# A batch's 24-point transform on VectorE and GpSimd: another table of steps, both DFT halves in one step, and half of the output subtraction a step sooner

## The chip, the cores and the metric

The kernel runs on one core of one Trainium2 chip. The metric is the device time of one execution in microseconds (us). The profiler's trace of one execution shows each instruction on TensorE (PE, with its weight loads as PEld), VectorE (DVE), ScalarE (ACT), GpSimd (POOL) and the DMA queues (SP issues most of them).

## What is computed

```python
X = np.fft.fft(np.fft.fft(x, axis=1), axis=2).real      # x: 8 x 3072 x 256
x = X.reshape(24576, 256)
h = x @ w_in                                            # w_in: 256 x 2048
x = (h - np.tanh(h)) @ w_out                            # w_out: 2048 x 256
logits = x @ w_gate                                     # 8 experts
out = gate * (relu(x @ w1[e]) @ w2[e])                  # e = argmax(logits), 256 -> 1024 -> 256
```

All of it is fp32; the kernel splits operands into a high and a low part (`hi`, `lo`) and multiplies hi by hi, hi by lo and lo by hi.

## The kernel before

Phase 1 (transform, first dense layer, gating, scattering the rows to the experts) takes some 1960 us, and phase 2 (the experts) the rest. The change touches phase 1 alone.

Phase 1 goes through 24 groups, three for each of the 8 batches; a group is 512 frequencies. A group has 18 steps (`NSTEP`), and the order of every engine's work is the order in which the program issues it. In a step `f` of group `g`:

- TensorE makes `u` and `v` of block `f` (`uv`, L419, 6 matmuls of 128x512), then adds the tanh part of block `f - 1` to four accumulators `acc[i, s]` (`tmm`, L466: 8 matmuls with `hi`, then 4 with `lo`). Steps 16 and 17 have no tanh block: there the last block's accumulation is done, half `i = 0` in step 16 and half `i = 1` in step 17. Step 0 has no `tmm`.
- VectorE makes `us` from `u` (`take_u`, L433), the low part `lo` of the second half of the previous block (`split_lo`, L460), and from `us` and `v` the two halves of `h` (`combine`, L438; in steps 16 and 17 they go into `lin`). `v` of the next step waits for these, since `u` and `v` have one bank each.
- ScalarE takes tanh of both halves twice, as `hi` and as `t` (`tanh`, L448). The second half's `t` goes to the PSUM bank m0 (then it is called `tp`), the first half's to SBUF.
- GpSimd makes the `lo` of the first half. From step 10 on it also finishes and scatters one block of rows of the group before (`rowS`, L601: a small copy and an indirect DMA), and in step 9 it converts the rows' places (`place`, L557), which VectorE computes at the end of that step.

Between groups, `out1(0)` and `out1(1)` (L481) subtract `acc` from `lin` on VectorE, two operations each; both stand in step 0 of the next group. The spectrum for group `g + 1` is made by `dft` (L351): two halves of 16 matmuls (128x128), each followed by a copy on ScalarE (`pqh`) and a subtraction on VectorE (`pql`). The halves stand in steps 0 and 1, and both use the PSUM bank m1; for group 1 they stand in steps 9 and 10 of group 0, and for group 3 in steps 14 and 15 of group 2.

A batch's 24-point transform (`fft_tasks`, L245) has to be done, in SBUF, before the `dft` of its first group. It is a list of operations: 24 pair operations of 128x768 (`two`), four multiply-adds of 128x768 on `y5, y4` and `y7, y6`, and four times `three`, each two operations of 128x512 and then 10 (once 4) smaller ones on VectorE. `when(nb)` (L55) says in which step each operation of batch `nb` is issued, at the end of the step; the dictionary `fq` holds them. From batch 2 on GpSimd does the pair operations and the first two of each `three`. For batch 1, VectorE does 12 of the pair operations and all of `three`. The transform of batch `nb` begins in group `3 nb - 5` and ends in group `3 nb - 2`, so in cycles of three groups; batch 1 has only groups 0 to 2 for it.

Of the kernel before, what the change touches and what calls it, by code (L numbers as in the profile page):

```python
# [9 lines left out]
F32 = mybir.dt.float32  # L10
# [10 lines left out]
P = 128  # L21
B, N, D = 8, 3072, 256
# [13 lines left out]
KF = FF // P  # L36
# [13 lines left out]
NCH = 3  # L50
NGRP = B * NCH
NSTEP = KF + 2


def when(nb):  # L55

    if nb == 1:
        steps = [t for t in range(12, 32) if t != 18]  # L60
        cut = [[32, 33], [33, 34], [37, 38, 39], [40, 42, 43], [44, 45, 46], [47, 48, 49]]
        return 8, [steps[i * 19 // 24] for i in range(24)], [(None, c) for c in cut]

    s = NSTEP * (NCH * nb - 5)
    slots = [s + NSTEP * g + t for g in range(4) for t in (0, 0, 1, 2, 3, 4, 5, 6, 7, 8, 9, 17)]

    slots = [t for t in slots if t >= s + (18 if nb == 2 else 6)]
    two, rest = slots[:18], slots[18:]
    r = two[-1] + 1
    six = [t for t in rest if t > r + 5][:6]  # L70
    q = six[-1] + 1
    end = s + 4 * NSTEP - 1
    half = (r + 6 + q + 1) // 2, (q + 1 + end) // 2
    return s + 1, two + six, [(None, [r, r + 1]), (None, [r + 2, r + 3]),
                              (r + 4, range(r + 5, half[0])), (r + 5, range(half[0], q + 1)),
                              (q, range(q + 1, half[1])), (q + 1, range(half[1], end))]


def parts(kb, ka):
# [108 lines left out]
def phase1(tc, a, bk, zscr, zny, base, small, ngrp=NGRP):  # L188
    nc = tc.nc
    V, S, G, T, Q = nc.vector, nc.scalar, nc.gpsimd, nc.tensor, nc.sync  # L190
    es = ExitStack()
    cp = es.enter_context(tc.tile_pool(name="cp", bufs=1))
    hp = es.enter_context(tc.tile_pool(name="hp", bufs=3))
# [5 lines left out]
    pm = es.enter_context(tc.tile_pool(name="pm", bufs=1, space=PSUM))  # L199
    free_banks = [(pm, "m0"), (pm, "m1")]  # L200
# [24 lines left out]
    tt = cp.tile([P, 2, 3, D], F32, name="tt")  # L225
# [16 lines left out]
        for i in parts:  # L242
            Q.dma_start(y[:, i:i + 5:4], a["x"][b - 1][:, i:i + 5:4])

    def fft_tasks(y, vs, tmp, eng, first=4):  # L245

        w = y.shape[-1]
        h = w // 2  # L250
        out = []

        def two(i, o0, o1, ops, src, k=0):
            e = eng(i, k)
            for o, x, op in zip((o0, o1), src, ops):
                out.append([(w, lambda o=o, x=x, op=op: e.tensor_tensor(o, *x, op))])

        pm_ops = (ALU.add, ALU.subtract)
        for b in range(4):
            t = tmp(b)  # L260
            yy = (y[:, b], y[:, b + 4])
            two(b, t[:, 0], t[:, 1], pm_ops, (yy, yy))
            o = y[:, b:b + 5:4]
            tf = (t[:, :, :, :h], t[:, :, :, h:])
            two(b, o[:, :, :, :h], o[:, :, :, h:], pm_ops, (tf, tf), 1)
        t = tmp(4)
        stt = V.scalar_tensor_tensor

        def each(*ops):
            out.append([(o.free_size(), lambda fn=fn, o=o, x=x: fn(o, *x)) for fn, o, *x in ops])  # L270

        halves = [(slice(0, h), -1.0), (slice(h, w), 1.0)]

        def three(kr, kj, real):
            sl = slice(kr, kj + 1, max(1, kj - kr))

            def x(i, r=None):
                if r is None:
                    return y[:, sl, i, :]
                return y[:, (kr, kj)[r], i, :]  # L280

            e = eng(9, kr)
            v = vs[(kr + 1) // 2 % 2]
            each((e.tensor_tensor, v, x(1), x(2), ALU.subtract), (e.tensor_tensor, x(1), x(1), x(2), ALU.add))
            f2 = [(stt, x(2), x(1), -0.5, x(0), ALU.mult, ALU.add)]
            if real:
                each(*f2, (V.tensor_tensor, x(0), x(0), x(1), ALU.add))
                each(*((V.tensor_scalar, x(1)[:, :, c], v[:, :, c], sg * S3, None, ALU.mult) for c, sg in halves))
                return
            each(*f2, (V.tensor_tensor, x(0, 0), x(0, 0), x(1, 0), ALU.add),  # L290
                 *((stt, x(0, 1)[:, c], x(0, 1)[:, c], sg, x(1, 1)[:, c], ALU.mult, ALU.subtract if sg < 0 else ALU.add)
                   for c, sg in halves))
            each((stt, x(1, 0), v[:, 1], -S3, x(2, 0), ALU.mult, ALU.add),
                 (stt, x(2, 0), v[:, 1], S3, x(2, 0), ALU.mult, ALU.add))
            each(*((stt, x(i, 1)[:, c], v[:, 0, c], (3 - 2 * i) * sg * S3, x(2, 1)[:, c], ALU.mult,
                    ALU.add if sg > 0 else ALU.subtract) for i in (1, 2) for c, sg in halves))

        sub = (ALU.subtract, ALU.subtract)
        s02, s13 = (y[:, 0], y[:, 2]), (y[:, 1], y[:, 3])
        d13 = (y[:, 5], y[:, 7])  # L300
        def two4():
            two(4, t[:, 0], t[:, 1], pm_ops[::-1], (d13, d13))

        if first == 4:
            two4()
        t5 = tmp(5)
        two(5, t5[:, 0], t5[:, 1], (ALU.add, ALU.add), (s02, s13))
        two(6, y[:, 0], y[:, 1], sub, (s02, s13))
        two(7, y[:, 2], y[:, 3], pm_ops, ((t5[:, 0], t5[:, 1]),) * 2)
        if first != 4:  # L310
            two4()

        each((stt, y[:, 5], t[:, 0], C8, y[:, 4], ALU.mult, ALU.add), (stt, y[:, 4], t[:, 0], -C8, y[:, 4], ALU.mult, ALU.add))
        each((stt, y[:, 7], t[:, 1], C8, y[:, 6], ALU.mult, ALU.add),
             (stt, y[:, 6], t[:, 1], C8, y[:, 6], ALU.mult, ALU.subtract))
        three(5, 7, False)
        three(4, 6, False)
        three(2, 3, True)
        three(0, 1, False)
        return out  # L320
# [127 lines left out]
    def tanh(hs, room):  # L448

        out = []  # L450
        for s in range(2):
            hi = sp.tile([P, 512], F32R, tag="hi", name=f"hi{s}")
            t = pm.tile([P, 512], F32, tag="m0", name="tp") if s and room else \
                hp.tile([P, 512], F32, tag=f"t{s}", name=f"t{s}", bufs=2 - s)
            S.activation(hi, hs[s], AF.Tanh)  # L455
            S.activation(t, hs[s], AF.Tanh)  # L456
            out.append((t, hi))
        return out
# [22 lines left out]
    def out1(i):  # L481
        for s in range(2):
            V.tensor_tensor(linb[s][:, i], linb[s][:, i], acc[i, s], ALU.subtract)  # L483
# [456 lines left out]
    z_parts = {0: 1, 2: 2, 4: 3}  # L940
    todo = []
    fq = {}

    th = hl = None
    for g in range(ngrp + 1):
# [2 lines left out]
        late = 0 if last else 2  # L948
        if last:
            free_banks.append((pm, "m0"))  # L950
        if g == 1:
            vvs = [vv, hp.tile([P, 2, D], F32, tag="t1", name="vv1", bufs=1)]
        for f in range(NSTEP):
            if last and f == 9:
                break
# [51 lines left out]
            if not last:  # L1007
                hs = combine(g, f, us, v)
                if g == 0:
                    rest(f, 2)  # L1010
                th = tanh(hs, g > 0 or f > 7) if f < KF else None
            if f == 0 and g > 0:
                out1(0)
                out1(1)
            for half in range(2):
                if nxt and f == ((9, 10) if g == 0 else (14, 15) if g == 2 else (0, 1))[half]:
                    dft(g + 1, half)()
            if g > 0:
                twin = (g - 1) % NCH == 0
                if f == late + 4:  # L1020
# [25 lines left out]

            now = NSTEP * g + f
            for nb in range(1, B):
                if nb * NCH < ngrp and now == when(nb)[0]:
                    load_x(nb)  # L1050
                    fft = fft_tasks(ys[nb], vvs if nb > 1 else [vv, vv], lambda i: tt,
                                    lambda i, k, nb=nb: V if nb == 1 and (i == 9 or i < 4 and k == 0 or i in (6, 7)) else G,
                                    4 if nb > 1 else 5)
                    _, pool, parts_at = when(nb)
                    for t, part in zip(pool, fft):
                        fq.setdefault(t, []).append(part[0][1])
                    rest_of = fft[24:]

                    cuts = [rest_of[:1], rest_of[1:2], rest_of[2:6], rest_of[6:10], rest_of[10:13], rest_of[13:]]
                    for (at, dve), part in zip(parts_at, cuts):  # L1060
                        steps = [x for p in part for x in p]
                        if at is not None:
                            fq.setdefault(at, []).extend(fn for _, fn in steps[:2])
                            steps = steps[2:]
                        size = sum(n for n, _ in steps)
                        done = 0
                        for n, fn in steps:
                            fq.setdefault(dve[done * len(dve) // size], []).append(fn)
                            done += n
            for fn in fq.pop(now, ()):  # L1070
                fn()
    es.close()
# [293 lines left out]
```

## Time and profile before

| | us |
|---|---|
| median of 3 runs | 3112.3 (3109.7 to 3113.9) |
| the profiled execution | 3112.51 |
| its span, first to last instruction | 3110.7 |
| TensorE busy | 3007.3 (97%) |
| VectorE busy | 2224.6 (72%) |
| ScalarE busy | 1632.0 (52%) |
| GpSimd busy | 1412.2 (45%) |

Busy shares are averages over both phases. Matmuls overlap in the records, so a TensorE that is busy can still be later than it need be: how long a group takes is read from the first `u` matmul of its step 0 to that of the next group. These starts cut the windows of the first view below.

### The profile page before, as it was taken

Reading aid. Unit: us, or ns where it says so; the run is one execution under the profiler, and the core shown is the slowest. Engines: PE = TensorE matmul, PEld = TensorE weight load, DVE = VectorE, ACT = ScalarE, POOL = GpSimd, SP = SyncE. Lnnn points to the kernel's source line nnn. Section 1 sums busy time; section 2 is a strip of 40 time slices with the busy share of each in tenths; the row PEclk is TensorE's granted clock in tenths of the full one; section 3 lists DMA queues with packets and bytes.
Section 4 is the critical chain, followed back from the end, with each engine's and each line's share of the span. In section 5 each row is a group of like instructions: output and inputs, shape, how many; then the busy total and the mean of one; then the engine's idle time right before and its main releaser. Section 6 shows DMA issues by size and latency. Waiting matters only on the chain. (4 is left out here: it accounts for less than half of the span.)

```text
span 3110.7 us, 44908 instructions
## 1 busy us (share of the span) xinstructions
PE 3007.3 (97%) x15660; PEld 2500.6 (80%) x15660; DVE 2224.6 (72%) x3925; ACT 1632.0 (52%) x3142; POOL 1412.2 (45%) x1372
## 2 busy tenths in 40 slices
PE   7998999999999999999999999799999999999998
PEld 7776778878778878878878887788888888888886
DVE  7779776777776776776776666776766767667664
ACT  4454545555545555555555555555555555555553
POOL 4466566566566566566554443622222222222222
PEclk8999999999999999999999999899999999999999
DMA  6120121121121121121111111765555556555551
GB/s 181 62 80 24 29 69 35 33 72 35 33 71 34 36 69 36 34 71 36 32 32 36 35 33 32 221 178 157 153 156 158 176 152 164 156 156 164 155 152 40
DMA packets 301614, 278.04 MB, mean 89 GB/s; under 512 B 246046, under 2 KB 261446, under 8 KB 285894
## 3 DMA queue, kind: packets, MB, share of 16 engines
q1 hardware_dynamic: 282422, 222.08, 26.7%
q0 software_dynamic: 18848, 52.99, 4.9%
q8 instruction: 125, 2.05, 0.3%
q14 instruction: 107, 0.88, 0.1%
q10 hardware_dynamic: 112, 0.05, 0.0%
HBM read 168.28 MB, written 55.39 MB: 72 GB/s over the span
## 5 line engine op out<-in xcount | busy, mean ns | idle before, releaser
L455 ACT ACTIVATE hi<-h 128x512 fp32r<-128x512 f32 x768 | 479.3, 624 | 835.9 <-DVE h L444 832.3
L463 POOL TENSOR_TENSOR lo<-t,hi 128x512 fp32r<-128x512 f32 x384 | 507.3, 1321 | 629.3 <-ACT t L456 500.1
L1290 POOL DMA_INDIRECT out_dram<-y,i x200 | 239.9, 1200 | 845.1 <-DVE y L1286 330.2
L435 DVE SCALAR_TENSOR_TENSOR us<-zb,A,u 128x512 f32<-128x512 f32 x432 | 321.8, 745 | 400.9 <-PE u L427 397.1
L1279 PE MATMUL dn<-w2s,hh 128*128 128x512 f32 x1600 | 572.3, 398 | 0.0
L1281 PE MATMUL dn<-w2s,hl 128*128 128x256 f32 x1600 | 449.2, 281 | 0.0
L1279 PEld LDWEIGHTS dn<-w2s,hh 128*128 128x128 f32 x1600 | 300.9, 188 | 69.5
L1266 PE MATMUL up<-xh,w1h 128*128 128x512 f32 (+1 forms) x960 | 344.7, 359 | 9.2 <-ACT xh L1254 9.2
L1267 PE MATMUL up<-xl,w1h 128*128 128x512 f32 (+1 forms) x960 | 341.7, 356 | 1.3 <-DVE xl L1255 1.1
L1268 PE MATMUL up<-xh,w1l 128*128 128x512 f32 (+1 forms) x960 | 342.5, 357 | 0.0
L1285 ACT ACTIVATE y<-dn,gi 128x256 f32<-128x256 f32 x200 | 95.1, 475 | 422.4 <-PE dn L1281 416.3
L1286 DVE SCALAR_TENSOR_TENSOR y<-dn,gi,y 128x256 f32<-128x256 f32 x200 | 96.8, 484 | 300.8 <-ACT y L1285 300.8
L1281 PEld LDWEIGHTS dn<-w2s,hl 128*128 128x128 f32 x1600 | 302.3, 189 | 4.9
L1271 DVE SCALAR_TENSOR_TENSOR hl<-up,hh 128x512 fp32r<-128x512 f32 (+1 forms) x480 | 271.7, 593 | 33.8 <-ACT hh L1270 33.8
L1270 ACT ACTIVATE hh<-up 128x512 fp32r<-128x512 f32 (+1 forms) x480 | 239.4, 521 | 94.1 <-PE up L1268 94.0
L444 DVE TENSOR_TENSOR h<-us,v 128x512 f32<-128x512 f32 x384 | 260.1, 677 | 3.0 <-DVE us L435 0.5
L445 DVE TENSOR_TENSOR h<-us,v 128x512 f32<-128x512 f32 x384 | 260.6, 679 | 0.0
L463 DVE TENSOR_TENSOR lo<-tp,hi 128x512 fp32r<-128x512 f32 x376 | 256.9, 683 | 3.7 <-ACT tp L456 3.7
L475 PE MATMUL acc<-hi,W0a 128*128 128x512 f32 x768 | 249.2, 405 | 0.4
L456 ACT ACTIVATE t<-h 128x512 f32<-128x512 f32 x392 | 241.4, 616 | 0.0
L479 PE MATMUL acc<-lo,W0a 128*128 128x512 f32 x768 | 215.8, 395 | 24.5 <-DVE lo L463 21.1
L475 PE MATMUL acc<-hi,W1a 128*128 128x512 f32 x768 | 238.9, 392 | 0.0
(278 smaller groups left out, 6516.6 us busy)
## 6 DMA issues: line engine op xcount, KB each, us to landing
w<-in_w SPq DMA_DIRECT2D x120, 1024.0 KB
yb<-in_x SPq DMA_DIRECT2D x16, 768.0 KB
ya<-in_x SPq DMA_DIRECT2D x12, 768.0 KB
zb<-zscr SPq DMA_DIRECT2D x24, 256.0 KB
raw<-in_win SPq DMA_DIRECT2D x8, 512.0 KB
raw<-in_wout SPq DMA_DIRECT2D x8, 512.0 KB
out_dram<-y,i POOLq DMA_INDIRECT x200
row<-pl SPq DMA_TRANSPOSE x184
```

The lines of the kernel that those rows point to most:

```text
L435: V.scalar_tensor_tensor(us, zb[g], A128[:, f:f + 1], u, ALU.mult, ALU.add)
L444: V.tensor_tensor(hs[0], us, v, ALU.subtract)
L445: V.tensor_tensor(hs[1], us, v, ALU.add)
L455: S.activation(hi, hs[s], AF.Tanh)
L463: e.tensor_tensor(lo, t, hi.bitcast(F32), ALU.subtract)
L475: T.matmul(acc[i, s], wout(wi, f)[:, c], hl[s][0], start=f == 0 and wi == 0, stop=False)
L1266: T.matmul(ps, w1h[:, k, c], xh[:, k], start=k == 0, stop=False)
L1267: T.matmul(ps, w1h[:, k, c], xl[:, k], start=False, stop=False)
L1268: T.matmul(ps, w1l[:, k, c], xh[:, k], start=False, stop=k == 1)
L1271: V.scalar_tensor_tensor(hl[:, m], ps, 0.0, hh[:, m].bitcast(F32), ALU.max, ALU.subtract)
L1279: T.matmul(ps.rearrange("p a d -> p (a d)"), hh[:, m, c], w2s[:, m].rearrange("p a d -> p (a d)"), start=m == 0, stop=False)
L1281: T.matmul(ps[:, 1], hl[:, m, c], w2s[:, m, 0], start=False, stop=m == 7)
```

## The change

The change replaces `when`, which worked out the steps by rules, by fixed lists of steps for batch 1, batch 2 and the batches from 3 on. From batch 3 on the pair operations stand in steps 17 and 0 to 9, and VectorE's operations in steps 10 to 14. For batch 2 VectorE's stand there too, but for four in steps 4 and 5 of group 3. For batch 1 GpSimd now does all pair operations and the first two of each `three`; VectorE's stand in steps 10 and 11 of group 1 and in steps 2 to 13 of group 2. The second buffer for `three` (`vv1`) is there from batch 1 on.

The second `dft` half moves from step 1 to step 0 and takes the bank m0, where the first keeps m1. For that, the second half's `t` of step 0 goes to SBUF. `out1(0)` moves from step 0 of the next group to step 17. Groups 0 and 2 keep their `dft` steps.

```diff
     if nb == 1:
-        steps = [t for t in range(12, 32) if t != 18]
-        cut = [[32, 33], [33, 34], [37, 38, 39], [40, 42, 43], [44, 45, 46], [47, 48, 49]]
-        return 8, [steps[i * 19 // 24] for i in range(24)], [(None, c) for c in cut]
...
-    return s + 1, two + six, [(None, [r, r + 1]), (None, [r + 2, r + 3]),
-                              (r + 4, range(r + 5, half[0])), (r + 5, range(half[0], q + 1)),
-                              (q, range(q + 1, half[1])), (q + 1, range(half[1], end))]
+        first = [12, 13, 14, 15, 16, 17, 17, 18, 18, *range(19, 28), 30, 32, 34, 35, 36, 36]
+        later = [(None, [28]), (None, [29]), (37, range(38, 41)), (38, range(41, 44)), (41, range(44, 46)), (44, range(46, 50))]
+        return [t + 36 for t in first], [(at and at + 36, [t + 36 for t in dve]) for at, dve in later]
+    if nb == 2:
+        return ([18, 18, 19, 20, 21, 22, 23, 24, 25, 26, 27, 35, 35, 36, 36, 37, 38, 39, 42, 43, 53, 53, 54, 54],
+                [(None, [40]), (None, [41]), (44, range(46, 49)), (45, range(48, 51)), (55, range(64, 66)), (56, range(66, 69))])
+    return ([4, 5, 6, 7, 8, 9, 17, 18, 18, 19, 20, 21, 22, 23, 24, 25, 26, 27, 37, 38, 39, 40, 41, 42],
+            [(None, [28, 29]), (None, [30, 31]), (35, range(46, 49)), (36, range(48, 51)),
+             (54, range(64, 66)), (55, range(66, 69))])
...
-            t = pm.tile([P, 512], F32, tag="m0", name="tp") if s and room else \
-                hp.tile([P, 512], F32, tag=f"t{s}", name=f"t{s}", bufs=2 - s)
+            if s and room:
+                t = pm.tile([P, 512], F32, tag="m0", name="tp")
+            elif s and room is None:
+                t = hp.tile([P, 512], F32, tag="t1", name="t1", bufs=1)
+            else:
+                t = hp.tile([P, 512], F32, tag="t0", name="t0", bufs=2)
...
-                th = tanh(hs, g > 0 or f > 7) if f < KF else None
+                th = tanh(hs, f > 0 if g > 0 else f > 7 or None) if f < KF else None
             if f == 0 and g > 0:
+                out1(1)
+            if f == NSTEP - 1 and not last:
                 out1(0)
-                out1(1)
             for half in range(2):
-                if nxt and f == ((9, 10) if g == 0 else (14, 15) if g == 2 else (0, 1))[half]:
+                if nxt and f == ((9, 10) if g == 0 else (14, 15) if g == 2 else (0, 0))[half]:
+                    if half and f == 0:
+                        free_banks[:] = [(pm, "m0")]
                     dft(g + 1, half)()
+                    free_banks[:] = [(pm, "m1")]
...
-                    fft = fft_tasks(ys[nb], vvs if nb > 1 else [vv, vv], lambda i: tt,
-                                    lambda i, k, nb=nb: V if nb == 1 and (i == 9 or i < 4 and k == 0 or i in (6, 7)) else G,
-                                    4 if nb > 1 else 5)
+                    if nb == 1:
+                        vvs = [vv, hp.tile([P, 2, D], F32, tag="t1", name="vv1", bufs=1)]
+                    first, later = when(nb)
+                    fft = fft_tasks(ys[nb], vvs, lambda i: tt, lambda i, k: G)
```

The numbers in the lists count steps from the first step of group `3 nb - 5`; for batch 1 this comes to steps of the whole kernel (18 is step 0 of group 1, 36 step 0 of group 2). VectorE's operations of a part are spread evenly over its steps, by their number.

## Rows read from the trace of the kernel before

**Rows 1.** Windows by group: start:end, length (us), busy times, clock, DMA share, GB/s:

```profile
166.40:245.50 79.10, 75.26 (x376) 60.33 (x375) 63.05 (x103) 40.63 (x76) 49.38 (x44) 1.00 0.23 71
245.50:336.00 90.50, 79.57 (x377) 61.14 (x378) 82.42 (x135) 40.89 (x77) 54.50 (x45) 0.98 0.11 28
336.00:413.70 77.70, 74.60 (x377) 60.66 (x375) 57.17 (x105) 40.62 (x76) 48.02 (x44) 1.00 0.13 32
413.70:645.10 231.40, 225.71 (x1128) 183.04 (x1127) 174.04 (x317) 122.02 (x229) 150.04 (x135) 0.99 0.17 46
645.10:1566.80 921.70, 900.66 (x4509) 730.62 (x4508) 674.88 (x1245) 487.97 (x916) 578.54 (x525) 1.00 0.17 46
1106.20:1185.80 79.60, 76.49 (x377) 61.86 (x376) 60.20 (x112) 40.62 (x76) 48.32 (x45) 0.98 0.25 71
1645.40:1869.30 223.90, 222.16 (x1129) 182.68 (x1128) 151.46 (x274) 122.02 (x229) 89.75 (x99) 1.00 0.14 33
```

**Rows 2.** Timeline, start of group 21: start us, us, instruction [idle before it]:

```profile
1723.23 0.48 PE L425 MATMUL u<-pqh,Mh 128*128 128x512 f32 x1
...
1723.09 2.47 DVE L483 TENSOR_TENSOR lin<-lin,acc 128x512 f32<-128x512 f32 x4
1726.08 0.73 DVE L435 SCALAR_TENSOR_TENSOR us<-zb,A,u 128x512 f32<-128x512 f32 x1
...
1727.47 0.97 PE L479 MATMUL acc<-lo,W0a 128*128 128x512 f32 x3 [0.56 <-DVE lo L463]
...
1724.77 0.58 ACT L361 ACTIVATE pqh<-dps 128x512 fp32r<-128x512 f32 x1
```

**Rows 3.** Timeline, end of group 12 and start of group 13:

```profile
1103.88 0.28 DVE L270 SCALAR_TENSOR_TENSOR yb<-yb 128x128 f32<-128x128 f32 x1
1106.46 4.03 DVE L270 SCALAR_TENSOR_TENSOR yb<-vv,yb 128x256 f32<-128x256 f32 x1
...
1104.80 1.87 POOL L256 TENSOR_TENSOR yb<-yb 128x768 f32<-128x768 f32 x1
1106.61 3.58 POOL L256 TENSOR_TENSOR yb<-tt 128x768 f32<-128x768 f32 x2
```

**Rows 4.** Timeline, group 2, steps 13 and 14:

```profile
312.82 0.39 PE L425 MATMUL u<-pqh,Mh 128*128 128x512 f32 x1
316.92 0.40 PE L425 MATMUL u<-pqh,Mh 128*128 128x512 f32 x1
321.25 0.96 PE L479 MATMUL acc<-lo,W0b 128*128 128x512 f32 x3 [0.70 <-DVE lo L463]
...
312.13 0.68 DVE L270 SCALAR_TENSOR_TENSOR yb<-yb 128x512 f32<-128x512 f32 x1
314.69 0.73 DVE L435 SCALAR_TENSOR_TENSOR us<-zb,A,u 128x512 f32<-128x512 f32 x1
317.15 2.79 DVE L270 SCALAR_TENSOR_TENSOR yb<-vv,yb 128x256 f32<-128x256 f32 x6
319.86 0.73 DVE L435 SCALAR_TENSOR_TENSOR us<-zb,A,u 128x512 f32<-128x512 f32 x1
...
312.95 1.47 POOL L463 TENSOR_TENSOR lo<-t,hi 128x512 fp32r<-128x512 f32 x1 [0.63 <-ACT t L456]
```

**Rows 5.** Timeline, step 10 of group 7:

```profile
697.56 1.20 PE L479 MATMUL acc<-lo,W0b 128*128 128x512 f32 x4 [0.66 <-POOL lo L463]
```

**Rows 6.** Groups by line, count | busy us, mean ns | idle us before:

```profile
L463 POOL TENSOR_TENSOR lo<-t,hi 128x512 fp32r<-128x512 f32 x384 | 507.3, 1321 | 629.3 <-ACT t L456 500.1 <-issue 103.7 <-POOL tt L256 13.1
L256 POOL TENSOR_TENSOR tt<-ya 128x768 f32<-128x768 f32 x36 | 66.8, 1865 | 1.1 <-DVE yb L270 0.9
L256 DVE TENSOR_TENSOR tt<-yb 128x768 f32<-128x768 f32 x8 | 7.4, 950 | 0.0
L591 POOL DMA_INDIRECT bk<-row,gpi x184 | 182.8, 994 | 52.5 <-POOL row L599 26.4 <-PE v L430 22.7 <-PE acc L475 1.8
L270 POOL TENSOR_TENSOR vv<-ya 128x512 f32<-128x512 f32 x12 | 15.5, 1295 | 3.1 <-DVE ya L270 3.1
```

More of the change, by code (lines that the diff above doesn't have):

```diff
@@ L59, in when @@
     if nb == 1:
-        steps = [t for t in range(12, 32) if t != 18]
-        cut = [[32, 33], [33, 34], [37, 38, 39], [40, 42, 43], [44, 45, 46], [47, 48, 49]]
-        return 8, [steps[i * 19 // 24] for i in range(24)], [(None, c) for c in cut]
[L64 to L73, printed above, removed]
-    return s + 1, two + six, [(None, [r, r + 1]), (None, [r + 2, r + 3]),
-                              (r + 4, range(r + 5, half[0])), (r + 5, range(half[0], q + 1)),
-                              (q, range(q + 1, half[1])), (q + 1, range(half[1], end))]
+        first = [12, 13, 14, 15, 16, 17, 17, 18, 18, *range(19, 28), 30, 32, 34, 35, 36, 36]
[7 more added lines that the diff above has]
+             (54, range(64, 66)), (55, range(66, 69))])
 def parts(kb, ka):
@@ L243, in load_x, with fft_tasks @@
             Q.dma_start(y[:, i:i + 5:4], a["x"][b - 1][:, i:i + 5:4])
-    def fft_tasks(y, vs, tmp, eng, first=4):
+    def fft_tasks(y, vs, tmp, eng):
         w = y.shape[-1]
@@ L300, in fft_tasks @@
         d13 = (y[:, 5], y[:, 7])
[L301 to L305, printed above, removed]
+        two(4, t[:, 0], t[:, 1], pm_ops[::-1], (d13, d13))
         t5 = tmp(5)
@@ L309, in fft_tasks @@
         two(7, y[:, 2], y[:, 3], pm_ops, ((t5[:, 0], t5[:, 1]),) * 2)
-        if first != 4:
-            two4()
         each((stt, y[:, 5], t[:, 0], C8, y[:, 4], ALU.mult, ALU.add), (stt, y[:, 4], t[:, 0], -C8, y[:, 4], ALU.mult, ALU.add))
@@ L942, in phase1 @@
     fq = {}
+    used = {}
     th = hl = None
@@ L950, in phase1 @@
             free_banks.append((pm, "m0"))
-        if g == 1:
-            vvs = [vv, hp.tile([P, 2, D], F32, tag="t1", name="vv1", bufs=1)]
         for f in range(NSTEP):
@@ L1048, in phase1 @@
             for nb in range(1, B):
-                if nb * NCH < ngrp and now == when(nb)[0]:
+                s = NSTEP * (NCH * nb - 5)
+                if nb * NCH < ngrp and now == max(8, s + 1):
                     load_x(nb)
-                    fft = fft_tasks(ys[nb], vvs if nb > 1 else [vv, vv], lambda i: tt,
-                                    lambda i, k, nb=nb: V if nb == 1 and (i == 9 or i < 4 and k == 0 or i in (6, 7)) else G,
-                                    4 if nb > 1 else 5)
[L1054 to L1061, printed above, removed]
+                    if nb == 1:
+                        vvs = [vv, hp.tile([P, 2, D], F32, tag="t1", name="vv1", bufs=1)]
+                    first, later = when(nb)
+                    fft = fft_tasks(ys[nb], vvs, lambda i: tt, lambda i, k: G)
+                    for t, fn in zip(first, (fn for part in fft[:24] for _, fn in part)):
+                        fq.setdefault(s + t, []).append(fn)
+                    for part, (at, dve) in zip((fft[24:25], fft[25:26], fft[26:30], fft[30:34], fft[34:37], fft[37:]), later):
+                        steps = [fn for p in part for _, fn in p]
                         if at is not None:
-                            fq.setdefault(at, []).extend(fn for _, fn in steps[:2])
+                            fq.setdefault(s + at, []).extend(steps[:2])
                             steps = steps[2:]
[L1065 to L1069, printed above, removed]
+                        for i, fn in enumerate(steps):
+                            fq.setdefault(s + dve[i * len(dve) // len(steps)], []).append(fn)
             for fn in fq.pop(now, ()):
```

## The prediction

> **What bounds the kernel now.** I read the windows by group first, then the timelines where a group is longer than its neighbours. TensorE is busy almost throughout, so phase 1 is as long as its matmuls and the waits between them; phase 2 is not touched. Three neighbouring groups without any transform take 223.9 us, 74.6 each. Groups 4 to 6, a first full cycle of a batch, take 231.4; each of the next four takes 921.7 / 4 = 230.4, and nearly all of its excess lies in one group: group 13 takes 79.6, so the other two take 150.8 together, only 1.6 over the plain ones. The first batch has group 1 at 79.1, group 2 at 90.5 and group 3 at 77.7 [rows 1]. What can be gained is these excesses, plus whatever wait a plain group still holds.
>
> A plain group holds one at its start. Step 1 begins at 1723.23, but its us comes only at 1726.08, 2.85 us later, since four subtractions (2.47 us) and pql go ahead of it; the lo matmul then waits for VectorE [rows 2]. How late is too late shows in group 2: in step 13 us comes at 314.69, 1.87 after the step's start at 312.82, and the next step still starts 4.10 later, an undisturbed step; in step 14 us comes 2.94 after the start, and TensorE waits with 0.70 of idle shown [rows 4]. I take the rule: a step loses what us comes later than 1.9 us after its start. For the plain step 1 that is 2.85 - 1.9 = 0.95.
>
> In a group like 13 it is worse. A 128x256 operation of VectorE at 1106.46 takes 4.03 us, because GpSimd operations at 1104.80 and 1106.61 (two, 3.58) run without a gap and it ends only after them [rows 3]. Everything at the group's start is then late.
>
> The Trainium skill (SBUF — State Buffer, "Who interferes with whom") says that a VectorE instruction with two SBUF inputs and a GpSimd instruction that reads SBUF block each other until the first finishes. The trace agrees that they block, but the 4.03 us reach past one GpSimd operation of 1.87 to the end of three. By that wording alone the wait would have been under 1.9 us, and the gain in each of six such groups some 2 us smaller.
>
> **The group's start after the change.** Edits: out1(0) goes to step 17, both DFT halves to step 0, no transform operation of VectorE in steps 15 to 17 and 0 to 9 from batch 3 on. TensorE's and VectorE's work stays the same, only its place changes. For a plain group I shift group 21's rows. Two of the four subtractions (1.24 us) run in step 17, in a gap of VectorE; us of step 0 then comes about 0.4 later, and the tanh chain 0.2 later. ScalarE's first pqh stood at 1724.77 and now at some 1724.9, the second follows at 1725.5, and their two pql end at about 1726.9, so that us of step 1 comes at 1726.85 [rows 2]. Step 1 itself begins 1.7 later (16 matmuls more in step 0), at 1724.9: us is 1.9 late, just inside the rule. Gain 0.95, of which I keep 0.9. Bounds: zero, if the second t, now in SBUF, makes lo wait for GpSimd; 0.95, if not. I take the upper end because the rows have GpSimd done with its pair operations by then. There are 19 such groups, 4 to 22: 17.1 us.
>
> Group 13's excess of 5.0 [rows 1] goes, but for two things. Step 10 still has a GpSimd pair operation behind the conversion of the places, which waits for VectorE: the lo after it comes late, at a loss of 0.9 in the trace (0.66 of it shown as idle) [rows 5]; I put 0.4 of it down to VectorE's operations in front of the conversion, which move away, and keep 0.5 (bounds 0.5 and 0.9). And lo of step 1 may stand behind the last GpSimd operation of three, 0.3. Gain 4.2, in six groups (4, 7, ... 19): 25 us.
>
> **The packed steps 10 to 14.** VectorE's operations start 2.46 after us (314.69 to 317.15) [rows 4]. With us 0.9 after an undisturbed start, they have 0.8 us before GpSimd's next lo, which then blocks them for about 1.1. The list of four (512, 256, 128, 128) is in rows 4: from 312.13 to 314.69, 2.56 us with the block, and us came 1.87 late, no loss. The change puts this list into step 10 of one group and step 12 of another: no loss. Step 12 of the third group gets three 128s in front of it, at 0.2 each (1103.88 and the operation behind it [rows 3]): 0.6 + 2.56 = 3.2, so us comes at 0.9 + 2.46 + 3.2 - 4.1 = 2.5, a loss of 0.6. I take 0.5. Bounds: 0, and 1.8 if a second GpSimd operation gets in between. The middle group keeps 0.4 at step 10. Both groups together stand at 0.9 over plain after, 1.6 before: gain 0.7 a cycle, five cycles, 3.5 us. The x load now has to land two steps sooner, by step 4; it is issued about a DFT half sooner, which I cost at nothing; if it came late, GpSimd's queue and the lo in it would stand still for as long.
>
> **The first batch.** GpSimd takes over 12 pair operations at 1.865 instead of 0.950 and 8 of 512 at 1.295 [rows 6]. In group 1 they fit beside lo (1.32): 79.1 becomes 73.7 plus 0.5 (step 10), 0.2 (two 768s in step 11) and 0.4 (lo of step 1 behind a pair operation), 74.8, a gain of 4.3. Group 3: four pair operations ahead of step 1's lo, so that VectorE's lo meets the fifth, 1.4; two of 1.295 behind the late conversion of step 9 and lo after them, done 4.2 into step 10 and wanted at 3.0, 1.2; steps 5 and 12, 0.7: 77.0, a gain of 0.7.
>
> Group 2 gets worse. From step 16 of group 1 GpSimd has queued: lo 1.3, two rows at 1.3 to 1.5 (the scatter alone is 0.994 [rows 6]), two pair operations, then four more in step 0: 15.5 us before the lo of step 1 can begin; with that lo it ends at 16.8. TensorE wants it after 2.7 + 2.9 + 1.4 for the three short steps, 1.3 of waits for VectorE and 3.3 within step 1: 11.6. Loss 5.2, and the 1.3. Steps 1 and 2 then carry 1.32 + 2 x 1.295 + 1.865 = 5.8 each against 4.1: with blocking by VectorE's operations 4.5 together. In steps 5 to 9 VectorE's lists lie again beside pair operations, each operation letting one of GpSimd pass: 9. Sum 20, and 1 for a clock that may fall in the first wait (in group 2 the windows show 0.98 already [rows 1]). On 74.0 that makes 95.5, 5 more than before. Bounds: 86, if the backlog drains as queued and VectorE's lists slip between; 104, if they don't. The three groups: -4.3 + 5.0 - 0.7 = 0. Groups 0 and 23 and the way into phase 2, where TensorE has Nyquist work beside the subtractions, stay.
>
> **Sum.** 17.1 + 25 + 3.5 + 0 = 45.6. The profiled execution took 3112.51, 0.2 above the median. 3112.5 - 45.5 = 3067.
>
> **The rivals.** *The start's wait stays.* The second t of step 0 in SBUF makes that lo a two-input operation, and it meets a GpSimd operation in most groups. For it: 4.03 us [rows 3]. Against: in the reckoning GpSimd is done just before. Price 0.95 in 19 groups and 0.5 more in half of them, 23 us: 3090.
>
> *The packed lists don't fit.* If each list also waits for the row's copy and scatter (0.99 [rows 6]) behind lo, a list of four loses 1.2 and the long one 2.5 or more: 5 a cycle, 25 us: 3092. Against: in step 13 of group 2 the last operations came before the scatter.
>
> *The slower engine's rule.* All of the added GpSimd time lies on the path: 12 x 0.915 + 8 x 0.6 = 16 us: 3083. For it: group 2. Against: GpSimd is busy 49 of 79 us in group 1 [rows 1]. The Trainium skill (GPSIMD Engine Reference, "Engine selection") gives this as a rule, elementwise work on VectorE, GpSimd being about two times slower for two inputs; the trace agrees on the ratio, 1.865 to 0.950.
>
> *Slower.* GpSimd becomes the bound at the group's start: in steps 17 and 0 it has rows and three pair operations before step 1's lo. By the rows' prices that lo ends some 2.4 us before TensorE wants it. Only if GpSimd is over 5 us later than that does each of 18 groups lose 2.6 and more, which eats all 46: 3114 to 3130.
>
> *No change.* The waits removed come back in steps 10 to 14 and group 2 in full: 3112.
>
> **Chances and range.** Forecast 0.64, start's wait 0.12, packed lists 0.09, slower engine's rule 0.06, slower 0.05, no change 0.04. About 0.2% (6 us) is what a measurement of this kernel can tell from no change: faster 0.91, same 0.04, slower 0.05. The forecast's own bounds: group 2 at 86 and no loss in step 12, 12 us less, to which I add 7 for the clock and starts that are better than plain: 3048. Upwards the first three rivals belong inside: 3094.
>
> **What would show it.** In the profile after: plain groups at 73.7, with the first lo matmul of step 1 not waiting; every third group at 74.5 instead of 79.6, and no VectorE operation of 4 us; step 12 before the last lists' group with a wait of about 0.5; group 2 longer than 90, its step 1 waiting 5 us for GpSimd. It is wrong if plain groups stay at 74.6, if a cycle stays above 226, or if group 2 is shorter than before.

## The result, and the profile after

The changed kernel takes 3067.24 us (median, 3065.23 to 3069.22) against 3111.0 of the kernel before beside it: a ratio of 0.9859, 95% interval 0.9842 to 0.9876. The forecast was 3067. The profiled execution took 3069.22 us with a span of 3067.4; of its 43.3 us less, 41.2 lie in groups 4 to 22, 0.9 in groups 1 to 3 and 1.2 behind group 22.

The windows of the changed kernel, columns as in [rows 1]: groups 1, 2, 3, then 7 to 18, 13, 14 and 15 alone, and 20 to 22.

```profile
166.40:241.10 74.70, 74.27 (x376) 60.53 (x375) 54.74 (x97) 40.52 (x76) 58.16 (x48) 1.00 0.24 73
241.10:336.90 95.80, 80.33 (x378) 61.79 (x377) 76.92 (x126) 41.04 (x77) 71.53 (x58) 0.96 0.12 28
336.90:412.80 75.90, 74.58 (x377) 60.53 (x376) 65.81 (x116) 40.50 (x76) 51.53 (x46) 1.00 0.15 33
636.80:1531.60 894.80, 890.90 (x4509) 728.81 (x4508) 677.67 (x1245) 486.78 (x916) 584.01 (x524) 1.00 0.18 48
1084.20:1158.90 74.70, 74.33 (x376) 60.56 (x375) 56.89 (x107) 40.57 (x76) 47.02 (x43) 1.00 0.26 75
1158.90:1233.30 74.40, 74.29 (x379) 61.02 (x379) 54.09 (x96) 40.65 (x77) 51.92 (x46) 1.00 0.16 34
1233.30:1308.00 74.70, 74.19 (x377) 60.63 (x376) 58.38 (x111) 40.52 (x76) 47.03 (x45) 1.00 0.15 34
1605.80:1827.20 221.40, 221.40 (x1129) 182.81 (x1129) 151.69 (x274) 121.69 (x229) 89.71 (x99) 1.00 0.15 34
```

Against [rows 1]: three plain groups 221.4 instead of 223.9, group 13 74.7 instead of 79.6, four cycles 894.8 instead of 921.7. Groups 1 to 3 take 246.4 together, 247.3 before: group 2 pays 5.3 of what groups 1 and 3 gain.

The start of group 21, which answers to [rows 2]: TensorE's first u and first lo matmul of step 1, VectorE's pql and us, ScalarE's pqh (start, us, idle before in brackets).

```profile
1684.63 0.48 PE L413 MATMUL u<-pqh,Mh 128*128 128x512 f32 x1
1687.90 1.07 PE L471 MATMUL acc<-lo,W0a 128*128 128x512 f32 x4
...
1685.33 1.29 DVE L350 TENSOR_TENSOR pql<-dps,pqh 128x512 fp32r<-128x512 f32 x2 [1.01 <-ACT pqh L349]
1686.54 0.74 DVE L423 SCALAR_TENSOR_TENSOR us<-zb,A,u 128x512 f32<-128x512 f32 x1
...
1684.72 1.06 ACT L349 ACTIVATE pqh<-dps 128x512 fp32r<-128x512 f32 x2
```

us comes 1.91 after the step's start, where it was 2.85, and the lo matmul waits for nothing. But ahead of pql VectorE is idle for 1.01: there it waits for ScalarE, no longer for the subtractions.

Three waits are left in the cycles. The first is step 10 of a group like 7, as in [rows 5]; GpSimd's conversion of the places, its pair operation and lo, and TensorE:

```profile
681.08 0.19 POOL L560 CAST gpi<-gpf 128x8 int32<-128x8 f32 x1 [3.37 <-DVE gpf L559]
681.23 1.86 POOL L250 TENSOR_TENSOR tt<-ya 128x768 f32<-128x768 f32 x1
683.03 1.30 POOL L455 TENSOR_TENSOR lo<-t,hi 128x512 fp32r<-128x512 f32 x1
...
684.38 1.20 PE L471 MATMUL acc<-lo,W0b 128*128 128x512 f32 x4 [0.28 <-POOL lo L455]
```

The second is the step 12 with seven operations, in group 15 and its like: VectorE's blocked operation, the next us, TensorE's first u and its wait in step 13.

```profile
1290.13 1.40 DVE L264 TENSOR_TENSOR ya<-ya 128x256 f32<-128x256 f32 x1
1291.85 0.73 DVE L423 SCALAR_TENSOR_TENSOR us<-zb,A,u 128x512 f32<-128x512 f32 x1
...
1289.17 0.39 PE L413 MATMUL u<-pqh,Mh 128*128 128x512 f32 x1
1293.24 0.97 PE L471 MATMUL acc<-lo,W0b 128*128 128x512 f32 x3 [0.52 <-DVE lo L455]
```

us is 2.68 late there; by the rule of 1.9 that loses 0.78. The blocked operation ends 0.29 after GpSimd's lo, which ran from 1289.62 to 1291.24.

The third is in step 1 of groups like 13. The second t of step 0 is in SBUF now, so VectorE's lo reads two SBUF operands there, and it meets a GpSimd operation of 128x512 that runs from 1090.89 to 1092.19:

```profile
1091.61 1.13 DVE L455 TENSOR_TENSOR lo<-t,hi 128x512 fp32r<-128x512 f32 x1
```

In a plain group this lo takes 0.68; step 1 is 0.4 longer in group 13 than in group 21.

In group 2, the end of GpSimd's chain across its start (two pair operations, and lo of step 1), and TensorE's wait in step 1:

```profile
247.10 3.90 POOL L250 TENSOR_TENSOR tt<-ya 128x768 f32<-128x768 f32 x2
250.96 1.25 POOL L455 TENSOR_TENSOR lo<-t,hi 128x512 fp32r<-128x512 f32 x1
...
252.27 2.07 PE L471 MATMUL acc<-lo,W0a 128*128 128x512 f32 x4 [4.67 <-POOL lo L455]
```

### The profile page after: what moved, and what is told of

Its sections match the earlier page's. It is cut to its first block, busy times and chain, and to the rows that moved or that the text cites. A ratio compares the mean times of both kernels' runs of the same rounds, so it can differ in the third digit from the quotient of the medians.

```text
span 3067.4 us, 44748 instructions
## 1 busy us (share of the span) xinstructions
PE 2988.3 (97%) x15660; PEld 2495.5 (81%) x15660; DVE 2210.4 (72%) x3905; ACT 1629.4 (53%) x3142; POOL 1444.4 (47%) x1392
## 5 line engine op out<-in xcount | busy, mean ns | idle before, releaser
L1281 POOL DMA_INDIRECT out_dram<-y,i x200 | 233.0, 1165 | 849.9 <-DVE y L1277 304.7
L448 ACT ACTIVATE t<-h 128x512 f32<-128x512 f32 x415 | 255.5, 616 | 3.4 <-POOL lo L455 3.4
L455 DVE TENSOR_TENSOR lo<-tp,hi 128x512 fp32r<-128x512 f32 x353 | 241.7, 685 | 7.3 <-ACT tp L448 6.7
L467 PE MATMUL acc<-hi,W0a 128*128 128x512 f32 x768 | 245.4, 400 | 0.0
L467 PE MATMUL acc<-hi,W0b 128*128 128x512 f32 x768 | 239.2, 393 | 0.0
L467 PE MATMUL acc<-hi,W1b 128*128 128x512 f32 x768 | 237.4, 390 | 0.0
```

The lines of the kernel that those rows point to most:

```text
L455: e.tensor_tensor(lo, t, hi.bitcast(F32), ALU.subtract)
L467: T.matmul(acc[i, s], wout(wi, f)[:, c], hl[s][0], start=f == 0 and wi == 0, stop=False)
```

## The experiments

**Which part brings what.** Four runs, beside one kernel before of 3110.15.

*e1_start*, the start alone, on the kernel before:

```diff
-                out1(0)
                 out1(1)
+            if f == NSTEP - 1 and not last:
+                out1(0)
...
-... (14, 15) if g == 2 else (0, 1))[half]:
+... (14, 15) if g == 2 else (0, 0))[half]:
```

> The kernel before with the edits of the group's start alone (both DFT halves in step 0, out1(0) in step 17, the second t of step 0 in SBUF); the transform's operations stay where they were. Theory A, the two parts of the change add up: the start's own wait of 0.95 goes in the groups whose start is free of transform work and the 4 us VectorE operations stay, 19 x 0.9 = 17 less, 3094, with group 21 at 73.7 and group 13 at 78 to 79. Rival B, the start gains only where the transform's operations have gone from it: groups 20 to 22 alone, 3 less, 3108.

3100.67 us, ratio 0.9961 (0.9947 to 0.9975): 9.5 less, between the two, with its five executions spread from 3093.98 to 3102.39. The windows of group 13 and of groups 20 to 22:

```profile
1099.50:1180.20 80.70, 76.63 (x377) 61.77 (x375) 60.59 (x112) 40.63 (x76) 48.58 (x45) 0.98 0.24 70
1637.60:1859.00 221.40, 221.40 (x1128) 182.67 (x1127) 151.77 (x274) 121.84 (x229) 90.00 (x99) 1.00 0.16 34
```

From the timeline, a VectorE operation at the start of its group 13:

```profile
1100.98 2.87 DVE L270 SCALAR_TENSOR_TENSOR yb<-vv,yb 128x256 f32<-128x256 f32 x1
```

Plain groups gain in full (221.4), but group 13 gets 1.1 longer than before instead of 0.9 shorter: the blocked operation ends at 1103.85, 4.35 into the group, as it did in [rows 3] (4.29), and everything of the start is in line behind it, now with both halves' pql. So the start's gain needs the lists where an operation of VectorE stands in the way, and only there.

*e2_lists*, the lists alone: the changed kernel with the start of the kernel before.

```diff
-                out1(1)
-            if f == NSTEP - 1 and not last:
                 out1(0)
+                out1(1)
...
-... (14, 15) if g == 2 else (0, 0))[half]:
+... (14, 15) if g == 2 else (0, 1))[half]:
```

> The changed kernel with the old start of a group (halves in steps 0 and 1, all four output subtractions in step 0); the new lists of steps stay. Theory A: the lists' share is 25 + 3.5, so 3111 - 28 = 3083; group 21 back at 74.6, groups like 13 at 75.5. Rival B, each part needs the other: less than 12 gained, 3099 or more, groups like 13 above 77.

3079.28 us, 0.9899 (0.9882 to 0.9915): 30.9 less, theory A. Groups 13, 14 with 15, and 20 to 22:

```profile
1085.20:1160.40 75.20, 74.34 (x376) 60.63 (x376) 56.53 (x107) 40.67 (x76) 47.12 (x43) 1.00 0.26 75
1160.40:1311.20 150.80, 148.99 (x753) 121.50 (x752) 112.27 (x206) 81.48 (x153) 99.06 (x89) 1.00 0.14 33
1611.70:1835.60 223.90, 222.13 (x1128) 182.60 (x1127) 151.37 (x274) 122.16 (x229) 89.99 (x99) 1.00 0.15 33
```

The plain groups are those of before to a tenth, and group 13 has lost 4.4 of its 5.0. Groups 14 and 15 take 150.8, as in the kernel before. The two parts alone give 40.4, together 43.8; with the spread of e1_start that difference of 3.4 is not shown by the times.

*e3_out1* and *e4_halves* split the start. The first puts out1(0) back into step 0:

```diff
             if f == 0 and g > 0:
+                out1(0)
                 out1(1)
-            if f == NSTEP - 1 and not last:
-                out1(0)
```

The second puts the DFT halves back into steps 0 and 1:

```diff
-... (14, 15) if g == 2 else (0, 0))[half]:
+... (14, 15) if g == 2 else (0, 1))[half]:
```

> The changed kernel with out1(0) back in step 0, so that all four output subtractions stand there with both DFT halves. Theory A: in the trace after, VectorE is idle between the last subtraction of step 0 and pql of step 1, which waits for ScalarE's pqh; four subtractions fit in front of it, and us of step 0 comes 0.4 sooner; so the same time within 5: 3062 to 3070, group 21 at 73.5 to 73.8. Rival B, the split is what frees VectorE: 0.9 is lost again in each of 19 groups, 3084, group 21 at 74.6.

> The changed kernel with the DFT halves back in steps 0 and 1 (and the second t of step 0 back in PSUM); out1(0) stays in step 17. Theory A: step 1 begins 1.7 sooner again while pqh still waits behind four tanh, so us of step 1 is 2.9 to 3.2 late and the start loses 0.95 to 1.3 in each of 19 groups: 3084 to 3090, group 21 at 74.6 to 74.9. Rival B, the split of the subtractions alone removes the wait: 3067 to 3070.

e3_out1 took 3063.79 us, 0.9853 (0.9837 to 0.9869); e4_halves 3085.88, 0.9923 (0.9906 to 0.9939). Theory A holds in both. Of e3_out1, the windows of groups 13 and 20 to 22:

```profile
1076.70:1151.00 74.30, 74.02 (x376) 60.56 (x375) 56.79 (x107) 40.64 (x76) 47.01 (x43) 1.00 0.27 76
1596.90:1818.10 221.20, 221.20 (x1128) 182.86 (x1127) 151.67 (x274) 121.88 (x229) 89.72 (x99) 1.00 0.16 34
```

The timeline of its start of group 21 (u of step 1 and us):

```profile
1675.70 0.48 PE L413 MATMUL u<-pqh,Mh 128*128 128x512 f32 x1
1677.37 0.74 DVE L423 SCALAR_TENSOR_TENSOR us<-zb,A,u 128x512 f32<-128x512 f32 x1
```

Of e4_halves, the window of groups 20 to 22:

```profile
1617.20:1841.80 224.60, 222.21 (x1128) 182.56 (x1127) 151.32 (x274) 122.01 (x229) 89.74 (x99) 1.00 0.17 33
```

And u of step 1 and us at its start of group 21:

```profile
1695.31 0.48 PE L413 MATMUL u<-pqh,Mh 128*128 128x512 f32 x1
1698.41 0.74 DVE L423 SCALAR_TENSOR_TENSOR us<-zb,A,u 128x512 f32<-128x512 f32 x1
```

With four subtractions in step 0 us is 1.67 late, sooner than the 1.91 of the changed kernel; with the halves apart 3.10, later than the 2.85 of before. The whole gain of the start comes from the second DFT half in step 0; moving out1(0) to step 17 brings nothing and pushes us of step 0, and so tanh and pqh, back. In groups like 13 that costs 0.4 (74.7 to 74.3): in e3_out1 VectorE's lo of step 1 is held up there too, but it begins 0.24 sooner and the step loses nothing. Lateness over 1.9 orders the plain groups in all four and gives their length to some 0.1: 0 (e3), 0 (changed), 0.95 (before), 1.2 (e4), with 73.7, 73.8, 74.6 and 74.9.

**The first batch.** *e5_batch1*: batch 1's list and engines as in the kernel before.

```diff
+        steps = [t for t in range(12, 32) if t != 18]
+        cut = [[32, 33], [33, 34], [37, 38, 39], [40, 42, 43], [44, 45, 46], [47, 48, 49]]
...
+... V if nb == 1 and (i == 9 or i < 4 and k == 0 or i in (6, 7)) else G
```

> The changed kernel with batch 1's transform as in the kernel before (its list, and VectorE again with 12 of the pair operations and all of three). Theory A, the prediction's bookkeeping for the first batch comes to nothing: group 1 at 77 (the start edit is in it now), group 2 at 91 to 93, group 3 at 77, the three together within 2 of the 246.4 of the changed kernel: 3065 to 3069. Rival B, moving the work to GpSimd was a net loss: group 2 falls by 5 and groups 1 and 3 stay, 3062. Rival C, it was a net gain: 3072 or more.

3063.09 us, 0.9852 (0.9836 to 0.9869), which the intervals don't tell from the changed kernel. In the profiled executions group 1 began between 159.7 and 166.4, whatever the lists, so from here on I compare lengths of groups. Groups 1 to 3:

```profile
161.30:238.50 77.20, 74.50 (x376) 60.46 (x375) 63.12 (x103) 40.52 (x76) 49.54 (x44) 1.00 0.23 73
238.50:330.10 91.60, 80.44 (x378) 61.87 (x379) 83.60 (x135) 40.93 (x77) 55.21 (x45) 0.96 0.12 27
330.10:405.90 75.80, 74.45 (x376) 60.46 (x375) 65.79 (x115) 40.51 (x76) 51.45 (x46) 1.00 0.14 33
```

Their sum is 244.6 against 246.4, within the 2 of theory A, though the time lies nearer to B: giving batch 1's work to GpSimd was worth nothing, and may have cost 2.

*e7_backlog*: batch 1's last four pair operations on VectorE, in group 1.

```diff
-        first = [... 30, 32, 34, 35, 36, 36]
+        first = [... 29, 31, 31, 32, 33, 34]
...
+... V if nb == 1 and i in (6, 7) else G
```

> The changed kernel with batch 1's four pair operations two6 and two7 on VectorE in steps 13 to 16 of group 1, and two5 on GpSimd in steps 11 and 13, so that nothing of batch 1 is queued on GpSimd at the end of group 1. Theory A, the loss of 6.9 in step 1 of group 2 is GpSimd's backlog: it falls below 1.5, and group 1 grows by 1 at most; 3061 to 3063. Rival B, the four operations on VectorE meet lo and the rows and make group 1 3 to 5 longer: 3065 or more. Rival C, step 1's loss is from something else and stays above 4.

3063.26 us, 0.9848 (0.9832 to 0.9864). The windows of groups 1 and 2:

```profile
160.80:237.80 77.00, 75.08 (x377) 60.36 (x376) 60.23 (x101) 40.51 (x76) 58.57 (x48) 1.00 0.23 71
237.80:330.60 92.80, 79.84 (x379) 61.03 (x378) 80.77 (x128) 40.92 (x77) 65.58 (x54) 0.98 0.12 29
```

TensorE's wait in step 1 of group 2, from the timeline:

```profile
249.91 1.19 PE L471 MATMUL acc<-lo,W0a 128*128 128x512 f32 x4 [0.98 <-POOL lo L455]
```

The wait falls from 4.67 to 0.98, so it was GpSimd's backlog. But group 2 gets only 3.0 shorter (later steps wait more), and group 1 gets 2.3 longer: the three groups take 245.7, 0.7 less. The cause is that of A; the price lies between A's 1 and B's 3 to 5.

**What was left in the cycles.** *e6_steps*: in step 9 the transform's operation ahead of the conversion, and VectorE's part of the second `three` one step later (shown for the batches from 3 on; batch 2's moves likewise).

```diff
                 if f == late + 7:
+                    for fn in fq.pop(now, ()):
+                        fn()
                     place(twin=twin)
...
-... (36, range(48, 51)), ...
+... (36, range(49, 52)), ...
```

> The changed kernel with two edits that the trace shows in different steps: in step 9 GpSimd's transform operation is issued ahead of the places' conversion, and the last list of the first two three parts begins one step later (49 to 51 instead of 48 to 50), so that no step 12 has seven operations. Theory A: the losses of 0.55 and 0.38 in step 10 go (1 a cycle) and the 0.75 in step 13 of every third group goes: 1.7 in six cycles, 10 less, 3057. Rival B: the conversion now waits behind the pair operation and step 10 loses as before, and the seven operations' loss comes back in steps 14 and 15: within 3 of 3067.

3055.51 us, 0.9822 (0.9805 to 0.9838). Groups 3, 13, and 14 with 15:

```profile
335.40:409.40 74.00, 74.00 (x376) 60.64 (x375) 65.95 (x115) 40.52 (x76) 50.73 (x46) 1.00 0.15 34
1075.50:1149.70 74.20, 74.12 (x377) 60.71 (x377) 56.89 (x108) 40.58 (x76) 47.25 (x44) 1.00 0.25 76
1149.70:1297.30 147.60, 147.60 (x753) 121.78 (x752) 112.38 (x206) 81.16 (x153) 97.95 (x89) 1.00 0.14 34
```

A cycle falls from 223.8 (74.7 + 74.4 + 74.7) to 221.8, group 3 by 1.9, and TensorE has no idle in groups 14 and 15. Group 1 is 1.1 longer (75.8): in steps 10 and 11 GpSimd's lo now comes sooner and meets VectorE's operations of 128x768, two of which take 1.94 and 1.95 us, where they took 0.96. Theory A: both waits were what they seemed.

*e10_both* joins e3_out1 and e6_steps; *e9_batch1* adds lists by hand for batches 1 and 2 (VectorE again with 12 of the pair operations, its other operations in steps 7 to 17 of group 1 and 10 to 15 of group 2; both DFT halves for group 3 in step 16 of group 2; batch 2 gets a list with one pair operation a step in group 2). Batch 1's has one step of the kernel for each operation:

```diff
+        return [12, 12, 13, 14, 15, 15, 16, 17, 19, 20, 20, 21, 21, 22, 22, 23, 24, 25, 27, 29, 29, 30, 31, 32,
+                25, 26, 27, 28, 28, 30, *[33] * 4, *[34] * 4, 35, 35, 31, 32, *[46] * 4, *[47] * 6,
+                36, 36, 48, 48, 49, 49, 48, 49, *[50] * 4, *[51] * 6]
```

> The edits of e3_out1 and e6_steps in one kernel; the first batch as in the changed kernel. Theory A, the two add up, 3 and 11: 3051 to 3054, with groups 4 to 19 between 73.7 and 74.0. Rival B, each hides the other's gain in part: 3056 or more.

> The kernel with the edits of e3_out1 and e6_steps, and a list by hand for the first two batches: batch 1's pair operations on both engines again, so that they end 4 steps sooner, GpSimd's operations of three one a step, nothing of VectorE's transform in steps 0 to 9 of group 2, the DFT for group 3 in step 16 of group 2, and batch 2 with one pair operation a step in group 2 (9, none in step 0). Theory A, the 20 us of group 2 are the two engines' lists lying on top of each other in steps 0 to 9: group 2 falls from 95.8 to 80 or less, groups 1 to 3 together from 246.4 to 232 or less, 3034 to 3040. Rival B, the work of the first batch bounds groups 1 and 2 whatever the order, and the loss only moves to other steps: the three together stay above 240, 3048 or more.

e10_both took 3055.32 us, 0.9825 (0.9809 to 0.9842); e9_batch1 3050.7, 0.982 (0.9803 to 0.9836), the shortest of all, though the intervals of the two don't part them. In e10_both, by its windows, groups 13 to 15 take 73.7 + 147.8 = 221.5, 0.3 less than in e6_steps: the two edits add up there, but 1.5 in five cycles is less than the times can show (3049.91 to 3057.02), so between A and B the times decide nothing; groups 5 to 19 lie where A put them, between 73.7 and 73.9, and group 4 at 74.8. Groups 1 to 3 of e9_batch1:

```profile
161.70:243.20 81.50, 76.09 (x377) 60.17 (x376) 73.54 (x112) 40.62 (x76) 54.31 (x46) 1.00 0.22 69
243.20:325.20 82.00, 77.09 (x379) 60.01 (x378) 66.30 (x119) 40.92 (x77) 58.42 (x50) 1.00 0.12 30
325.20:406.00 80.80, 76.43 (x376) 60.08 (x375) 66.88 (x115) 40.63 (x76) 54.29 (x47) 1.00 0.18 31
```

Group 2 falls from 95.8 to 82.0, but group 1 rises to 81.5 and group 3 to 80.8: 244.3. Rival B. Four lists for the first batch (changed, e5, e7, e9) give 246.4, 244.6, 245.7 and 244.3; with the other edits of e9_batch1 the changed kernel's list takes 245.4 (e10_both). The loss moves from group to group; whether another order would remove it stays open.

**What a blocked VectorE operation waits for.** *e8_probe* has an extra operation ahead of out1(0) in step 17:

```diff
+            if f == NSTEP - 1 and g in (7, 13, 19, 21, 22):
+                V.tensor_tensor(probe, probe, probe, ALU.max)
+            if f == NSTEP - 1 and g in (10, 16):
+                V.tensor_scalar(probe, probe, 1.0, None, ALU.mult)
```

*e11_gap* is the same with the list shifted by one operation, so that the second pair operation of the chain has to wait for the first:

```diff
-    return ([4, 5, 6, 7, 8, 9, 17, 18, 18, 19, 20, ...
+    return ([4, 5, 6, 7, 8, 9, 9, 17, 18, 18, 19, ...
```

> The changed kernel with one extra 128x256 operation of VectorE at the end of step 17, ahead of out1(0): with two SBUF inputs in groups 7, 13, 19, 21 and 22, a tensor_scalar with one input in groups 10 and 16. In groups 7, 10, 13 and 16 GpSimd then runs three pair operations back to back, the first of them already under way. Theory A, a blocked VectorE operation waits through the whole chain: 4 to 4.5 us in groups 7 and 13, ending with the third pair operation, and step 1 of the next group 3 to 4 late. Rival B, it waits for the one that is running: 0.5 to 1.3 us, next to nothing lost. Groups 21 and 22 have no pair operation there, 0.3 to 0.4 us by both. The one-input operation: 0.2 to 0.4 us if it doesn't share a port with GpSimd, as long as the other if it does.

> The kernel of e8_probe with the list of the batches from 3 on shifted by one operation, so that the pair operation of step 17 reads tt and the next one, in step 0, writes it and has to wait for it. In e8_probe the first two pair operations ran into each other without a gap (706.20 to 709.85) and the third began 0.08 later; the VectorE operation, ready at 707.61, ended at 710.14. Theory A, a blocked VectorE operation waits until GpSimd's operations leave a gap: here the gap stands behind the first, so the operation in groups 7 and 13 takes 0.7 to 1.0 us and the start of groups 8 and 14 loses less than 0.6. Rival B, it waits for the running operation and the one queued behind it, gap or not: 2.5 us as in e8_probe, and the start of groups 8 and 14 loses 2.4.

The one execution of e8_probe took 3074.96 us, that of e11_gap 3079.39 (its shifted list puts two pair operations into step 9, whose lo is then late in step 10). Of e8_probe GpSimd's pair operations at the end of group 7, the probe there, and the one-input probe of group 10:

```profile
706.20 3.65 POOL L250 TENSOR_TENSOR ya<-tt 128x768 f32<-128x768 f32 x2
709.93 1.89 POOL L250 TENSOR_TENSOR tt<-ya 128x768 f32<-128x768 f32 x1
...
707.61 2.53 DVE L1009 TENSOR_TENSOR probe<-probe 128x256 f32<-128x256 f32 x1
...
933.82 2.38 DVE L1011 TENSOR_SCALAR probe<-probe 128x256 f32<-128x256 f32 x1
```

And of e11_gap:

```profile
708.20 1.87 POOL L250 TENSOR_TENSOR ya<-tt 128x768 f32<-128x768 f32 x1
710.15 3.70 POOL L250 TENSOR_TENSOR tt<-ya 128x768 f32<-128x768 f32 x2
...
709.61 0.75 DVE L1009 TENSOR_TENSOR probe<-probe 128x256 f32<-128x256 f32 x1
...
937.47 0.61 DVE L1011 TENSOR_SCALAR probe<-probe 128x256 f32<-128x256 f32 x1
1762.84 0.42 DVE L1009 TENSOR_TENSOR probe<-probe 128x256 f32<-128x256 f32 x1
```

In e8_probe neither theory is right: the probe passes over the end of the first pair operation, which the second follows without a gap (two in 3.65), and ends 0.29 after the second (709.85), though a third follows 0.08 later (709.93). In e11_gap the gap of 0.08 (710.07 to 710.15) stands behind the first, and the probe ends 0.29 after that. The last row is group 22, without pair operations. So the operation waits for the first gap, not for one operation and not for the whole chain; in [rows 3] three ran without one. The tensor_scalar with one SBUF input is held up nearly as long in both; no run shows its time undisturbed.

## Why the prediction was right, and where not

**The total.** That 3067 was met to 0.3 is in part luck. The sum took 45.5 off the profiled 3112.5; the change brought 43.8, from 3111.0. In the profiled executions groups 4 to 22 gave 41.2 where 45.6 was put down, and 2.1 came from places that were put at nothing: 0.9 from groups 1 to 3 and 1.2 from behind group 22, where the runs differ by as much (1239.4 to 1242.0).

**The start.** 223.9 - 221.4 = 2.5 for three plain groups, 0.83 each where 0.9 was kept: 16 us in 19 groups for 17.1. The rule of 1.9 and the time of us (1.9 late by reckoning, 1.91 measured) held. The reason was half wrong: the prediction laid the wait to the four subtractions and pql ahead of us. Its own rows have pqh end at 1725.35, 0.2 before the subtractions do (1725.56) [rows 2], so that moving these could bring 0.2 at most, and by e3_out1 and e4_halves it brings nothing; in the changed kernel pql waits for pqh. The time was right because the part that counts, 16 matmuls more ahead of step 1, was in it too.

**Groups like 13.** 79.6 to 74.7 is 4.9; without the start 4.1, predicted 4.2. The two waits left are those named, the step 10 that e6_steps removes and a late lo in step 1, 0.4 where 0.3 was put down. But that lo is VectorE's, held up because its t is in SBUF now. e2_lists, with this t in PSUM, shows what the lists do alone: 4.4.

**The packed steps.** This is the term that was mis-sized: a gain of 0.7 a cycle was predicted. Four cycles gained 26.9, or 6.7 each; less 3 x 0.83 and 4.1 that leaves 0.1, so 3 of the 4.4 us by which groups 4 to 22 fell short of 45.6. e2_lists shows the term by itself: groups 14 and 15 take 150.8 there, as before the change. The list of four lost nothing, as predicted. The seven operations of step 12 lost 0.78 where 0.5 was taken: a 128x256 operation took 1.40 there against lo, and us came 2.68 late instead of 2.5. With it, groups 14 and 15 keep 74.4 + 74.7 - 2 x 73.8 = 1.5 over plain groups, where 0.9 was put down; before it was 1.6.

**The first batch.** Groups 1, 2 and 3 were put at 74.8, 95.5 and 77.0 (the terms given for group 2 add up to 95.0); they took 74.7, 95.8 and 75.9. The backlog was the right cause (e7_backlog), and that the batch's new division brings nothing held too (e5_batch1). Group 3 was put 1.1 too long: its step 1 lost nothing, where 1.4 was put down. In group 2 errors cancel, so that its sum is luck in part. The clock, for which 1 was put down, cost some 2.5: behind the wait of 4.67 the four lo matmuls of step 1 take 2.07, not 1.07 as in group 21, and step 2 takes 5.6 us instead of 4.1 with TensorE busy throughout, at a granted clock of 0.71, so for part of it at 1.2 GHz instead of 2.4. Its window:

```profile
254.15:259.77 5.62, 5.62 (x19) 4.51 (x18) 4.07 (x6) 2.10 (x4) 5.54 (x5) 0.71 0.00 0
```

Step 3 takes 6.5, so 2.4 is left for GpSimd's added work of steps 1 and 2, which was put at 4.5; steps 6 to 10, behind the lists put at 9, lose 9.9.

**The rivals.** The start's wait did not stay; but what that rival named, a lo with two SBUF operands that meets GpSimd, does happen in the groups like 13, for 0.4 each. No packed list but the long one lost time, and nothing came later than TensorE wanted it at a plain group's start. The slower-engine rule gave 3083; beside e5_batch1, which leaves that work on VectorE, the first three groups took 1.8 more, not 16. Which waits the longer operations took the place of, no run parts.

**One step held for a reason that was not quite it.** The prediction read 4.03 us as the time to the end of three GpSimd operations and set it against the Trainium skill (SBUF — State Buffer, "Who interferes with whom"), by which the second one blocks until the first finishes. The runs show a third reading, until the first gap, which in [rows 3] is the end of the three: 2.53 us in e8_probe, 0.75 in e11_gap. The same section counts tensor_scalar, in its 2-port modes, among the operations that can contend with GpSimd. The one-input probe agrees that it contends, 2.38 us; in which mode it ran, no run shows.

## What to carry to other kernels

Before an operation is moved to clear a path, look which input of the late instruction comes last: here the subtractions were visibly in the way, and yet only giving TensorE more to do ahead of the step helped. A packed step is judged by how late the next step's first instruction on the engine becomes, against the lateness that the trace shows to be free. When three rearrangements move a loss from group to group and the sum stays within some 2 us, the next gain is elsewhere: two small moves in the steady cycles gave 2 us in each.

## What was not expected of the hardware

A VectorE operation with two SBUF inputs is not let in between two GpSimd operations that follow each other without a gap, but a gap of 0.08 us is enough: 2.53 us for a 128x256 operation that takes 0.42 undisturbed, 0.75 when the gap came one operation sooner.
